# Order and pace of weight conversion and eviction in the two out products of an attention and two-MLP kernel

## The chip, the cores and the metric

The kernel runs on one core of a Trainium2 chip. The metric is the device time of one execution in microseconds; the median of three runs stands for a kernel. The trace is of one profiled execution. TensorE is called PE, VectorE DVE, ScalarE ACT, GpSimd POOL, SyncE SP.

## The reference

Sparse attention (8 heads, 2 batches of 768 positions, head size 64) is followed by two feed-forward blocks over the 1536 tokens. Only the feed-forward blocks matter here:

```python
x = attn_out.reshape(1536, 512)
xn = x / sqrt(mean(x * x) + 1e-6) * rms_g
g = xn @ w_gate                              # 512 -> 1536
x = (g * sigmoid(g) * (xn @ w_val)) @ w_out  # 1536 -> 512, the first out product
r = maximum(x @ moe2_w_in, 0)                # 512 -> 2048, the in product
out = (s * (r * r) + b) @ moe2_w_out         # 2048 -> 512, the second out product
```

The weights `w_gate`, `w_val`, `w_out`, `moe2_w_in` and `moe2_w_out` come as 64-bit words that the kernel converts itself.

## The kernel before, in words

Tokens are taken in NB = 3 blocks ("batches" in the code, index b) of 512. The width of the inner layers is taken in pieces of 128 (index f): F1 = 12 pieces for the first block, F2 = 16 for the second. Each float32 operand is split into a high and a low part, and one product is three matmuls (`mm3`, lines 183 to 186): high by high, high by low, low by high.

After the attention, `Mlp.run` goes through four stages, each a list of steps of 12 matmuls of 128x128 by 128x512:

- the gate and value products (lines 478 to 489), two steps for each (f, b);
- the first out product, weights named "o" (lines 499 to 515): 36 steps, b outermost, f inside, as `order1` says;
- the in product, weights "i" (lines 539 to 551): 48 steps, f outermost, b inside;
- the second out product, weights "p" (lines 571 to 584): 48 steps in the order of `order2`, b outermost, f inside.

A step of an out product needs three things: the converted weight of its f (`self.get`), four PSUM banks that add up over all f of one b (`acc`, banks "a" for b = 0 and 2, "gv" for b = 1), and the split of its activation tile: `split1` and `split2` write the high part on ACT and the low part on DVE. The split of step n + 1 is issued behind the matmuls of step n. It has two buffers (`side` and `ev`), which take turns, so the split of step n + 1 can begin only when step n - 1 is through on PE.

After each step, `tick(gap)` advances the weights that are in conversion by one stage each, and starts a new weight if `gap` steps have gone by since the last start. The work of one weight of 128x512 (`stages`, lines 255 to 295, in the order of `steps`) takes four ticks: (1) magnitude on ACT, floor on DVE; (2) shifts and low on DVE; (3) high on DVE, which also sets the raw buffer free and issues the load of a later weight on SP's queue; (4) `hi_part` on ACT and `lo_part` on POOL. There are three raw buffers (`raw`) and three work buffers (`cv`). Converted weights go to a ring of 8, or to a pool of their own (o with f < 4, p with f >= 8). A weight for the ring waits until an older one is dropped: in the first out product this happens in its last batch only, and so the "i" weights start at step 28 of 36. The pool for p with f >= 8 opens when the second out product begins, and so these 8 weights are converted inside that stage.

Evictions of finished sums are put off by `later(d, ...)`: to the d-th tick from there. `evac1` writes one PSUM bank as a high part (ACT) and a low part (DVE); `evac2` copies one bank to SBUF (even t on DVE, odd t on ACT) and issues its store on SP's queue.

Each engine runs its instructions in the order in which this code issues them.

Of the kernel before, what the change touches and what calls it, by code (L numbers as in the profile page):

```python
# [23 lines left out]
F1, F2 = DFF1 // 128, DFF2 // 128  # L24
BLK = 512
HB = 256
NB = B * S // BLK
# [29 lines left out]
def kernel(  # L57
# [104 lines left out]
    def open_psum(e):  # L162
        psum[:] = [e(tc.tile_pool(name="psum", bufs=1, space=PSUM))]

    def ps(kind):
        m = banks[kind][turn[kind] % len(banks[kind])]
        turn[kind] += 1
        return psum[0].tile([128, 512] if m < 8 else [128, 2, 512], F32, name=f"ps{m}", tag=f"b{m}")
# [14 lines left out]
    def mm3(o, ahi, alo, bhi, blo, first, last):  # L183
        T.matmul(out=o, lhsT=ahi, rhs=bhi, start=first, stop=False)  # L184
        T.matmul(out=o, lhsT=ahi, rhs=blo, start=False, stop=False)  # L185
        T.matmul(out=o, lhsT=alo, rhs=bhi, start=False, stop=last)  # L186


    class Mlp:
# [267 lines left out]
        def run(self, done):  # L457
            rS = ExitStack()
            open_psum(rS.enter_context)

            p1S = ExitStack()
            self.p1 = p1S.enter_context(tc.tile_pool(name="p1", bufs=NB * (F1 - G0), side="right"))
            yw = p1S.enter_context(tc.tile_pool(name="yw", bufs=F1 - RING, side="right"))
            self.xpool["o"] = (yw, lambda f: f < F1 - RING)
            parts = {}
            order1 = [(b, f) for b in range(NB) for f in range(F1)]
            y = {}

            ev1 = p1S.enter_context(tc.tile_pool(name="ev1", bufs=1, side="right"))

            def split1(n):
                b, f = order1[n]
                pt = self.pt.pop((f, b))
                phi, plo = parts[n] = self.split_tiles(n, ev1)
                A.activation(phi, pt, AF.Copy)
                V.tensor_sub(plo, pt, phi.bitcast(F32))

            for f in range(F1):
                for b in range(NB):
                    left = [c for c in (0, HB) if (f, 2 * b + c // HB) not in done]  # L480
                    if not left:
                        continue
                    c0, c1 = left[0], left[-1] + HB
                    if f == F1 - 1 and b == NB - 1:
                        split1(0)
                    for fn in self.gate_val(f, b, c0, c1, lambda: ps("gv")[:, : c1 - c0]):
                        self.later(1, fn)
                        self.tick()
                self.drop("g", f), self.drop("v", f)

            def evac1(acc, yy, m):
                yhi, ylo = yy
                A.activation(yhi[:, m, :], acc[m], AF.Copy, scale=0.5)
                V.scalar_tensor_tensor(
                    ylo[:, m, :], in0=acc[m], scalar=0.5, in1=yhi[:, m, :].bitcast(F32), op0=ALU.mult, op1=ALU.subtract
                )

            self.flush()
            for n, (b, f) in enumerate(order1):
                if f == 0:  # L500
                    acc = [ps("a" if b % 2 == 0 else "gv") for _ in range(4)]
                hi, lo = self.get("o", f)
                phi, plo = parts.pop(n)
                for m in range(4):
                    ms = slice(m * 128, (m + 1) * 128)
                    mm3(acc[m], hi[:, ms], lo[:, ms], phi, plo, f == 0, f == F1 - 1)
                if b == NB - 1:
                    self.drop("o", f)
                if n + 1 < len(order1):
                    split1(n + 1)  # L510
                if f == F1 - 1:
                    y[b] = self.new_xy()
                    for m in range(4):
                        self.later(1 + m // 2, lambda acc=acc, b=b, m=m: evac1(acc, y[b], m))
                self.tick(1)
            self.flush()
            p1S.close()
            self.p0S.close()

            gS = ExitStack()  # L520
            gp = gS.enter_context(tc.tile_pool(name="gp", bufs=NB * F2, side="right"))
            gt = {}

            def act2(o, g):
                r = self.side()
                A.activation(r, o, AF.Relu)  # L526
                V.scalar_tensor_tensor(g, in0=r, scalar=s_col, in1=r, op0=ALU.mult, op1=ALU.mult)  # L527

            def split2(n, ev=None):
                b, f = order2[n]  # L530
                g = gt.pop((f, b))
                phi, plo = parts[n] = self.split_tiles(n, ev)
                A.activation(phi, g, AF.Identity, bias=b_col)  # L533
                V.scalar_tensor_tensor(plo, in0=g, scalar=b_col, in1=phi.bitcast(F32), op0=ALU.add, op1=ALU.subtract)  # L534

            order2 = [(b, f) for b in range(NB) for f in range(F2)]
            order = [(f, b) for f in (0, 1) for b in (0, 1)] + [(0, 2), (1, 2)]
            order += [(f, b) for f in range(2, F2) for b in range(NB)]
            for f, b in order:
                hi, lo = self.get("i", f)  # L540
                yhi, ylo = y[b]
                o = ps("gv")
                for kk in range(KD):
                    mm3(o, hi[:, kk, :], lo[:, kk, :], yhi[:, kk, :], ylo[:, kk, :], kk == 0, kk == KD - 1)
                g = gt[(f, b)] = gp.tile([128, BLK], F32, name="gt", tag="gt")
                self.later(1, lambda o=o, g=g: act2(o, g))
                if b == NB - 1:
                    self.drop("i", f)
                if (f, b) == order[-1]:
                    split2(0)  # L550
                self.tick()

            self.flush()
            self.xyS.close()
            with (
                tc.tile_pool(name="ow", bufs=F2 - RING) as ow,
                tc.tile_pool(name="ev2", bufs=1, side="right") as ev2,
                tc.tile_pool(name="ob", bufs=4, side="right") as ob,
            ):
                self.xpool["p"] = (ow, lambda f: f >= RING)  # L560

                def evac2(acc, b, t):
                    o = ob.tile([128, BLK], F32, name="o", tag="o")
                    if t % 2:
                        A.activation(o, acc[t], AF.Copy)
                    else:
                        V.tensor_copy(o, acc[t])
                    r0 = self.row_of[4 * b + t]
                    nc.sync.dma_start(out[r0 : r0 + 128, :], o)

                for n, (b, f) in enumerate(order2):
                    if f == 0:
                        acc = [ps("a" if b % 2 == 0 else "gv") for _ in range(4)]
                    hi, lo = self.get("p", f)
                    phi, plo = parts.pop(n)
                    for t in range(4):
                        ts = slice(t * 128, (t + 1) * 128)
                        mm3(acc[t], phi[:, ts], plo[:, ts], hi, lo, f == 0, f == F2 - 1)
                    if n + 1 < len(order2):
                        split2(n + 1, ev2)  # L580
                    if f == F2 - 1:
                        for t in range(4):
                            self.later(1 + t // 2, lambda acc=acc, b=b, t=t: evac2(acc, b, t))
                    self.tick(1)
                self.flush()
            gS.close()
            rS.close()
# [554 lines left out]
```

## Time and profile before

| what | value |
|---|---|
| median of 3 runs | 678.24 us (677.86 to 679.38) |
| the profiled execution | 677.87 us |
| its span, first to last instruction | 676.1 us |
| PE busy | 657.4 us, 97% of the span |
| DVE busy | 408.9 us, 60% |
| ACT busy | 277.4 us, 41% |
| POOL busy | 161.1 us, 24% |
| mean granted TensorE clock | 0.995 |

Matmuls overlap, so a matmul is listed with some 390 ns although a new one begins every 227 ns. The length of a step, from its first matmul to the first of the next, is therefore a better measure than the busy time.

### The profile page before, as it was taken

What the parts mean: (1) busy time and instruction counts of PE and PEld (TensorE: products, weight loads), DVE (VectorE), ACT (ScalarE), POOL (GpSimd) and SP (SyncE); (2) the same over time, 40 slices, a digit from 0 to 9 for tenths busy, and PEclk for the clock granted to TensorE, in tenths of its full rate; (3) what the DMA queues carried; (4) which work ended last, traced back from release to release, by engine and by line L of the source; (5) the groups of instructions that cost most, each with busy time, mean ns of one, the idle gap of its engine ahead of it and who ended that gap; (6) DMA issues with size and microseconds to landing.
All of it is one profiled execution on the core that took longest, in us unless ns stands there. A gap on an engine that the chain in (4) does not pass through costs nothing.

```text
span 676.1 us, 9146 instructions
## 1 busy us (share of the span) xinstructions
PE 657.4 (97%) x3380; PEld 538.1 (80%) x3380; DVE 408.9 (60%) x847; ACT 277.4 (41%) x580; POOL 161.1 (24%) x137
## 2 busy tenths in 40 slices
PE   8999999999999999999999999999999998999996
PEld 5688888878888888888888878888888766888885
DVE  6779976336675557776324497765666798323322
ACT  3898788313332223343323344333333544322321
POOL 2476677302221112222000042211111134000000
PEclk9899999999999999999999999999999999999998
DMA  5775431003221123333000043321111231100101
GB/s 180 226 216 178 147 111 63 1 1 94 93 94 62 63 64 101 105 103 96 0 1 1 22 134 93 95 62 63 63 62 63 78 126 47 64 0 1 63 0 66
DMA packets 39940, 52.47 MB, mean 78 GB/s; under 512 B 5072, under 2 KB 31696, under 8 KB 39888
## 3 DMA queue, kind: packets, MB, share of 16 engines
q1 hardware_dynamic: 39216, 51.56, 24.1%
q8 instruction: 28, 0.46, 0.3%
q10 hardware_dynamic: 672, 0.26, 0.1%
q14 instruction: 24, 0.20, 0.1%
HBM read 48.67 MB, written 3.15 MB: 77 GB/s over the span
## 4 chain that ended last, share of the span: by engine, by line
PE 81%; DVE 8%; ACT 5%; DMA 2%; issue 2%; POOL 0%; SPq 0%; ACTq 0%; DVEq 0%; POOLq 0%
PE ps L186 26%; PE ps L184 26%; PE ps L185 25%; ACT t L810 3%; PE ps L853 1%; PE ps L782 1%; DVE t L795 1%; DVE u L277 1%; PE ps L834 1%; DMA kw<-in_k_dram 1%; DVE sm L816 1%; DVE u L271 1%; DVE ev L534 1%; DMA raw_i<-in_moe_w_in_dram 1%; DMA raw_p<-in_moe_w_out_dram 1%
## 5 line engine op out<-in xcount | busy, mean ns | idle before, releaser
L184 PE MATMUL ps<-xyh,hi_i 128*128 128x512 f32 x192 | 74.7, 389 | 0.0
L185 PE MATMUL ps<-xyl,hi_i 128*128 128x512 f32 x192 | 74.7, 389 | 0.0
L186 PE MATMUL ps<-xyh,lo_i 128*128 128x512 f32 x192 | 74.7, 389 | 0.0
L527 DVE SCALAR_TENSOR_TENSOR gt<-side,sb 128x512 f32<-128x512 f32 x48 | 38.7, 806 | 39.6 <-ACT side L526 39.6
L184 PE MATMUL ps<-xyh,hi_g 128*128 128x512 f32 (+1 forms) x160 | 60.3, 377 | 1.1 <-DVE p L924 1.1
L184 PE MATMUL ps<-xyh,hi_v 128*128 128x512 f32 (+1 forms) x160 | 60.0, 375 | 0.1
L526 ACT ACTIVATE side<-ps 128x512 f32<-128x512 f32 x48 | 28.7, 597 | 76.5 <-PE ps L186 76.5
L185 PE MATMUL ps<-xyl,hi_v 128*128 128x512 f32 (+1 forms) x160 | 58.8, 368 | 0.0
L185 PE MATMUL ps<-xyl,hi_g 128*128 128x512 f32 (+1 forms) x160 | 58.8, 368 | 0.0
L186 PE MATMUL ps<-xyh,lo_v 128*128 128x512 f32 (+1 forms) x160 | 58.8, 368 | 0.0
L186 PE MATMUL ps<-xyh,lo_g 128*128 128x512 f32 (+1 forms) x160 | 58.8, 368 | 0.0
L439 ACT ACTIVATE side<-ps 128x512 f32<-128x512 f32 x30 | 17.9, 598 | 99.1 <-PE ps L186 99.1
L290 POOL TENSOR_TENSOR lo_i<-u,hi_i 128x512 fp32r<-128x512 f32 x16 | 22.9, 1432 | 139.3 <-ACT hi_i L286 130.5
L810 ACT ACTIVATE t<-t,mn 128x232 f32<-128x232 f32 (+1 forms) x96 | 44.2, 464 | 13.0 <-DVE mn L795 12.9
L271 DVE TENSOR_SCALAR u<-u 128x512 int32<-128x512 int32 x68 | 48.7, 717 | 0.0
L821 POOL TENSOR_TENSOR t<-t,sm 128x928 f32<-128x928 f32 (+1 forms) x24 | 41.4, 1725 | 24.5 <-DVE sm L817 20.9
L440 DVE SCALAR_TENSOR_TENSOR side<-side,ps 128x512 f32<-128x512 f32 x30 | 20.6, 688 | 43.0 <-ACT side L439 43.0
L185 PEld LDWEIGHTS ps<-xyl,hi_i 128*128 128x128 f32 x192 | 36.0, 188 | 7.5
L184 PEld LDWEIGHTS ps<-xyh,hi_i 128*128 128x128 f32 x192 | 36.0, 188 | 7.5
L268 DVE TENSOR_SCALAR u<-u 128x512 f32<-128x512 f32 x68 | 39.3, 580 | 4.3 <-ACT u L264 4.3
L186 PEld LDWEIGHTS ps<-xyh,lo_i 128*128 128x128 f32 x192 | 36.0, 188 | 7.4
L534 DVE SCALAR_TENSOR_TENSOR ev<-gt,sb,ev 128x512 fp32r<-128x512 f32 x24 | 19.0, 793 | 35.0 <-ACT ev L533 35.0
(138 smaller groups left out, 1533.0 us busy)
## 6 DMA issues: line engine op xcount, KB each, us to landing
raw_i<-in_moe_w_in_dram SPq DMA_DIRECT2D x16, 512.0 KB, 3.7
raw_p<-in_moe_w_out_dram SPq DMA_DIRECT2D x16, 512.0 KB, 3.5
raw_g<-in_moe_w_gate_dram SPq DMA_DIRECT2D x12, 512.0 KB, 3.6
raw_v<-in_moe_w_val_dram SPq DMA_DIRECT2D x12, 512.0 KB, 3.6
raw_o<-in_moe_w_out_dram SPq DMA_DIRECT2D x12, 512.0 KB, 3.5
vw<-in_v_dram SPq DMA_DIRECT2D x10, 512.0 KB, 3.5
out_dram<-o SPq DMA_DIRECT2D x12, 256.0 KB, 2.3
q<-in_q_dram SPq DMA_DIRECT2D x11, 256.0 KB, 5.5
```

What stands on the lines that cost most here:

```text
L184: T.matmul(out=o, lhsT=ahi, rhs=bhi, start=first, stop=False)
L185: T.matmul(out=o, lhsT=ahi, rhs=blo, start=False, stop=False)
L186: T.matmul(out=o, lhsT=alo, rhs=bhi, start=False, stop=last)
L268: e.tensor_scalar(u, u, 2.0**-15, None, op0=ALU.max)
L271: V.tensor_scalar(ui, ui, 5, 2, op0=ALU.logical_shift_left, op1=ALU.logical_shift_right)
L290: e.tensor_tensor(lo, u, hi.bitcast(F32), op=ALU.subtract)
L440: V.scalar_tensor_tensor(th[:, :w], in0=th[:, :w], scalar=1.0, in1=g, op0=ALU.add, op1=ALU.mult)
L526: A.activation(r, o, AF.Relu)
L527: V.scalar_tensor_tensor(g, in0=r, scalar=s_col, in1=r, op0=ALU.mult, op1=ALU.mult)
L534: V.scalar_tensor_tensor(plo, in0=g, scalar=b_col, in1=phi.bitcast(F32), op0=ALU.add, op1=ALU.subtract)
L810: A.activation(t[:, hh, :], t[:, hh, :], AF.Exp, bias=mn[:, hh : hh + 1], scale=-1.0, accum_out=sm[:, hh : hh + 1])
L821: e.tensor_tensor(t, t, st["sm", g].unsqueeze(2).to_broadcast([128, 4, W]), op=ALU.mult)
```

## The change

Three things are edited, all in `Mlp.run`. In the first out product, a weight conversion starts at every second step at most in place of every step (`tick(2)`), and the four banks of a batch are evicted one at a step in place of two. In the second out product, `order2` runs f = 0 to 7 of batch 0, then f = 0 to 7 of batch 1, then f = 8 to 15 of batch 0, then f = 8 to 15 of batch 1, then all f of batch 2; the sums of batches 0 and 1 are kept in `accs` while both are open; and a conversion starts at every second step at most. The eviction of the second out product stays at two banks a step (one on each of ACT and DVE).

```diff
@@ first out product
                 if f == F1 - 1:
                     y[b] = self.new_xy()
                     for m in range(4):
-                        self.later(1 + m // 2, lambda acc=acc, b=b, m=m: evac1(acc, y[b], m))
-                self.tick(1)
+                        self.later(1 + m, lambda acc=acc, b=b, m=m: evac1(acc, y[b], m))
+                self.tick(2)
@@ second out product
-            order2 = [(b, f) for b in range(NB) for f in range(F2)]
+            order2 = [(b, f) for fs in (range(F2 // 2), range(F2 // 2, F2)) for b in (0, 1) for f in fs]
+            order2 += [(b, f) for b in range(2, NB) for f in range(F2)]
+            accs = {}
...
                     if f == 0:
-                        acc = [ps("a" if b % 2 == 0 else "gv") for _ in range(4)]
+                        accs[b] = [ps("a" if b % 2 == 0 else "gv") for _ in range(4)]
+                    acc = accs[b]
...
-                    self.tick(1)
+                    self.tick(2)
```

## Rows read from the trace of the kernel before

**Rows 1.** Busy time of PE in the page's first part.

```profile
PE 657.4 (97%) x3380; PEld 538.1 (80%) x3380; DVE 408.9 (60%) x847; ACT 277.4 (41%) x580; POOL 161.1 (24%) x137
```

**Rows 2.** Windows by stage; columns: stretch, length, busy by engine, clock, DMA.

```profile
200.00:301.99 101.99, 101.99 (x452) 84.45 (x450) 63.98 (x102) 30.78 (x53) 19.51 (x16) 1.00 0.25 81
301.99:402.11 100.12, 99.35 (x434) 80.87 (x432) 52.23 (x79) 35.58 (x61) 13.00 (x8) 1.00 0.15 44
402.11:532.67 130.56, 130.56 (x578) 108.11 (x576) 87.08 (x122) 48.81 (x86) 23.39 (x18) 1.00 0.23 72
532.67:572.12 39.45, 35.57 (x145) 26.25 (x144) 36.20 (x50) 19.68 (x32) 14.39 (x10) 1.00 0.29 94
572.12:670.20 98.08, 98.08 (x433) 80.89 (x431) 30.05 (x41) 28.17 (x40) 0.17 (x1) 1.00 0.07 24
```

**Rows 3.** Windows by step, first out product: steps 1, 33, 34, 35.

```profile
304.71:307.77 3.06, 3.01 (x14) 2.17 (x12) 3.06 (x5) 1.83 (x3) 1.28 (x1) 1.00 0.24 58
...
392.09:395.05 2.96, 2.88 (x13) 2.06 (x11) 2.93 (x5) 1.25 (x3) 1.68 (x1) 1.00 0.39 104
395.05:398.75 3.70, 3.29 (x13) 2.18 (x13) 3.67 (x7) 1.71 (x4) 1.82 (x1) 1.00 0.49 147
398.75:402.11 3.36, 3.13 (x13) 2.36 (x13) 3.33 (x6) 1.37 (x3) 1.83 (x1) 1.00 0.41 116
```

**Rows 4.** Windows by step, second out product: steps 1, 5, then 6 to 11.

```profile
535.39:538.82 3.43, 3.04 (x13) 2.18 (x12) 3.40 (x7) 1.28 (x3) 0.02 (x1) 1.00 0.00 0
...
546.98:549.70 2.72, 2.72 (x13) 2.25 (x12) 2.69 (x5) 1.83 (x3) 0.32 (x2) 1.00 0.30 81
549.70:553.21 3.51, 2.90 (x13) 2.06 (x11) 3.29 (x6) 1.33 (x3) 1.34 (x1) 1.00 0.43 121
553.21:556.53 3.32, 3.26 (x12) 2.10 (x12) 3.29 (x4) 1.82 (x4) 1.33 (x1) 1.00 0.34 138
556.53:560.55 4.02, 3.29 (x13) 2.10 (x12) 3.99 (x7) 1.80 (x4) 1.78 (x1) 1.00 0.48 140
560.55:564.29 3.74, 3.32 (x12) 2.10 (x12) 3.71 (x6) 1.81 (x4) 1.51 (x1) 1.00 0.36 130
564.29:567.67 3.38, 3.13 (x13) 2.28 (x13) 3.35 (x5) 1.72 (x3) 1.53 (x2) 1.00 0.00 0
567.67:572.12 4.45, 3.02 (x13) 2.18 (x12) 3.25 (x4) 1.35 (x2) 2.56 (x2) 1.00 0.01 2
```

**Rows 5.** Instructions on the raw tiles of p: ns min/median/max, first, last start.

```profile
L264 ACT ACTIVATE u<-raw_p x16: 657/668/687, 476.8 to 562.9; 128x512 f32<-128x512 f32 x16
L274 DVE SCALAR_TENSOR_TENSOR u<-raw_p,u x16: 691/693/694, 480.3 to 567.3; 128x512 int32<-128x512 int32 x16
L277 DVE SCALAR_TENSOR_TENSOR u<-raw_p,u x16: 677/686/1783, 482.5 to 569.6; 128x512 int32<-128x512 int32 x16
...
DMA to landing us min/median/max: 3.4/3.5/4.3
```

**Rows 6.** Timelines of ACT, DVE and POOL, 538.7 to 572.2: start, length, instruction, wait.

```profile
562.95 0.68 ACT L264 ACTIVATE u<-raw_p 128x512 f32<-128x512 f32 x1 [1.93 <-DMA raw_p<-in_moe_w_out_dram]
563.09 0.41 DVE L271 TENSOR_SCALAR u<-u 128x512 int32<-128x512 int32 x1
564.14 0.42 DVE L268 TENSOR_SCALAR u<-u 128x512 f32<-128x512 f32 x1
564.15 0.62 ACT L286 ACTIVATE hi_p<-u 128x512 fp32r<-128x512 f32 x1
564.48 0.74 DVE L534 SCALAR_TENSOR_TENSOR side<-gt,sb,side 128x512 fp32r<-128x512 f32 x1
567.66 1.45 POOL L290 TENSOR_TENSOR lo_p<-u,hi_p 128x512 fp32r<-128x512 f32 x1 [1.29 <-ACT hi_p L286]
567.89 1.77 DVE L534 SCALAR_TENSOR_TENSOR ev<-gt,sb,ev 128x512 fp32r<-128x512 f32 x1
572.15 0.72 ACT L533 ACTIVATE ev<-gt,sb 128x512 fp32r<-128x512 f32 x1 [1.23 <-PE ps L185]
```

## The prediction

> **What bounds the kernel now.** I read the page's busy times first: PE is busy for 657.4 us, 97% of the span [rows 1]. A change that keeps the number of matmuls can win only where PE stands still, so the next view is the windows by stage, to see where that is. The in product is the yardstick: its 48 steps take 130.56 us with PE busy all the time, 2.72 us a step of 12 matmuls, at a granted clock of 1.00, the upper level of 2.4 GHz [rows 2]. Against it, the first out product's 36 steps should take 97.92 us and take 100.12, 2.20 too many. The second one's steps 0 to 11 should take 32.64 us and take 39.45, 6.81 too many; its later 36 steps take 98.08, within 0.2 us of 36 x 2.72 = 97.92 [rows 2]. The gate and value stage before them has PE busy all the time. So the stages that the change touches hold 2.20 + 6.81 = 9.01 us of standstill, 1.3% of the time, and no more can be won.
>
> The windows by step put a place on each part. In the first out product four steps are over 2.72: step 1 by 0.34, and steps 33, 34 and 35 by 0.24, 0.98 and 0.64 [rows 3]; they add up to the whole 2.20, so all other steps, those with evictions too, lose nothing. In the second, step 1 loses 0.71, and steps 6 to 11 lose 0.79, 0.60, 1.30, 1.02, 0.66 and 1.73, together 6.10 [rows 4]. These are the steps in which one weight after another is converted.
>
> Why they lose is a count of DVE's work. One weight costs DVE floor 0.42, shifts 0.41, low 0.69 and high 0.69, 2.21 us in all, and the split of the step 0.74 [rows 5, 6]: 2.95 us, more than a step of 2.72 has, when a weight goes through in every step. POOL makes it worse: a `lo_part` ran from 567.66 for 1.45 us, and the split that DVE began 0.23 us later took 1.77 us in place of 0.74; `high` has a median of 0.69 and a longest of 1.78 [rows 5, 6]. The third part is the load: it is issued by `high` and lands 3.5 us later (median), longer than a step; ACT's magnitude waited 1.93 us for it at 562.95, and the split's ACT half stands behind it in ACT's queue [rows 5, 6]. In the losing steps DVE is busy for 3.25 to 3.99 us of 3.32 to 4.45 [rows 4].
>
> **The change part by part.** *Pace in the second out product.* No instruction is added or removed; the 8 weights p8 to p15 are spread from a start in every step (1 to 8) to a start in every second step (1, 3, to 15). I followed the code's ticks by hand. p8 is finished at step 4 as before, p15 at step 18 (before: 11). The new order needs p8 at step 16, and p15 at step 23: a margin of 5 steps at the least, where the old order would have needed p15 at step 15. So the slower pace is paid for by the new order, and `get` never has to force a conversion.
>
> What a pair of steps now holds, from its start at 0: ACT's split half 0 to 0.72, DVE's half to 1.46; ACT's `hi_part` 0.72 to 1.34, so POOL's `lo_part` 1.34 to 2.79; DVE's shifts begin at 1.46, stand behind POOL until 2.79 and end at 3.20, low at 3.89; in the second step ACT's half runs 2.72 to 3.44 and DVE's half 3.89 to 4.63, then high to 5.32 and floor to 5.74 [rows 5, 6]. Each split is ready before its step must begin (1.46 against 2.72, 4.63 against 5.44), by 1.26 and 0.81 us. The DVE sum with the standstill is 2.21 + 2 x 0.74 + 1.33 = 5.02 of 5.44 us. Loads have four steps, 10.9 us, from `high` to the magnitude that needs them, against 3.5 [rows 5], so ACT's queue is clear as well. Steps 6 to 11 lose nothing any more: minus 6.10.
>
> Step 1 stays. Up to it the two versions issue the same instructions in the same order on every engine: the split of step 1 goes out at step 0, behind the last ReLU and square of the in product and p7's magnitude and floor. Its 0.71 us remains [rows 4].
>
> *Pace in the first out product.* At step 28 the ring frees its first place. Before, a weight starts in each of steps 28 to 35; now at 28, 30, 32 and 34. That is the same pair of steps as above, so steps 33 to 35 lose nothing: minus 1.86 [rows 3]. The bill goes to the in product, which finds three weights converted at its start in place of five. It needs weight f at step 3f (from f = 2 on), and gets i3 at step 1, i4 at 3, then one every second step: i3 with 8 steps to spare, and more for each later one. That stage carries 87 us of DVE work in 130.56 [rows 2] and more of it moves to its first 22 steps; its PSUM banks take turns by four, which hides a late eviction for 3 steps, some 8 us. I cost it at nothing; without that cover, each late step would cost like those of rows 4, 0.6 to 1.7 us. From its step 22 on both versions issue the same. Step 1 of this stage stays too (0.34): the split that it waits for is queued before the two versions differ. Weights o10 and o11 are finished by step 5 and needed at step 10.
>
> *Evictions of the first out product.* Four pairs of ACT and DVE instructions are spread from two steps to four. The steps that hold them lose nothing now, since the four steps listed carry the stage's whole 2.20 us [rows 3], so nothing is won. In the last batch three of the four now come in the `flush` ahead of the in product, ahead of its first evictions; they are read by the in product's step 4, 10.9 us later. Cost nothing.
>
> *Order and banks.* Batches 0 and 1 hold all eight banks from step 8 to step 23. The "gv" banks were last used by the in product, whose last eviction is issued at step 0; batch 2 takes "a" at step 32, 8 steps after batch 0 was evicted. Batch 0's stores go out at steps 23 and 24 in place of 15 and 16; on SP's queue they now follow the loads of all weights, the last of which moves from step 7 to 11. Batch 1's and batch 2's stores, and so the tail of the kernel, stay where they were. Whether a sum that is left half done for 8 steps costs PE anything, no row shows. The nearest one is that banks change every three matmuls now at no cost, in 2.72 us steps [rows 2], so I take nothing.
>
> *Sum.* 6.10 + 1.86 = 7.96 us go, 1.05 stay. The profiled execution took 677.87 (its span is 676.1, and 1.8 lies around it): 677.87 - 7.96 = 669.91. The median of the runs lies 0.37 higher than this execution, so I say 670.1, between the two bases. Bounds of what is unsure: at best the two step 1 stalls go as well, 677.87 - 9.01 = 668.9. At worst a pair of steps is less clean than worked out; the smallest standstill of rows 3 and 4, 0.24 us, for each of the 11 weights converted beside splits (p8 to p15, i0 to i2) is 2.6 us: 672.5. I take nothing for it, because step 5 of the second out product holds 2.69 us of DVE work in 2.72 and loses nothing [rows 4].
>
> **A rule against it.** The row of 567.89 shows DVE held until POOL is through [rows 6]. The Trainium skill (SBUF — State Buffer, section "SBUF: two separate sides") states why: the port pair of GpSimd and VectorE is an exclusive lock, held for a whole instruction, and the loser blocks fully, as VectorE operations with two SBUF inputs do. By that rule the change lifts no lock: each weight still has its `lo_part`, whatever the pace. The trace agrees (1.77 for 0.74). By the row alone the lock is one step's accident and the sum stays 669.9; by the rule it can come back with every weight, which is the slower rival below.
>
> **The rivals.** *The lock takes the split, and it is slower.* If POOL's `lo_part` begins before DVE's split, the split is held, and PE waits for it: step 11 lost 1.73 that way [rows 4, 6]. At 11 weights this is 19.0 us, and 677.87 - 7.96 + 19.0 = 688.9. It decides from 7.96 / 11 = 0.72 us a weight. For it speaks that the lock is seen; against it that `hi_part`, and so `lo_part`, stands behind the split's ACT half in ACT's queue, 0.62 us after it, and that DVE has 0.4 us to spare in a pair of steps.
>
> *The lock takes a part.* Half of the slower price, or the mean of the nine standstills (0.88) for the 8 weights p8 to p15, is 7.1 us: 677.0. Between this and 672.5 lies a lock that hits some weights alone.
>
> *It doesn't do what it says.* If ACT's wait for the loads sets the second stage [rows 6] and does so at any pace, only the 1.86 of the first goes: 676.0. Against it: the wait stands because `high` is late and the next magnitude comes one step behind, which the new pace ends.
>
> **How the numbers follow.** The forecast (669.3 to 671) has 0.75. A start without the step 1 stalls, 668.9: 0.04. The lock in part: 0.12, about half of it below 672.5. Not as it says, 676.0: 0.05. Slower, 688.9: 0.04. The range 668.8 to 672.5 holds some 0.85. Within 0.2% (1.4 us, about what a measurement of this kernel can tell from no change) lies only the end of the partial lock, 0.03; faster 0.93, slower 0.04.
>
> **What would show it.** In the trace of after: windows by step of 2.72 for steps 2 to 23 of the second out product, and for steps 28 to 35 of the first; step 1 still at 3.4 and 3.1; no wait of ACT for a raw tile of p; the in product at 130.6 in all, as before. A split of 1.8 us with a step over 3 us behind it would speak for the lock, an in product over 131 for weights or evictions that come late, a step 16 or later over 2.72 for conversions that the new order needs too early.

## The result, and the profile after

The changed kernel takes 668.51 us (668.41 to 669.33) beside 678.05 us of the kernel before, a ratio of 0.9872 with a 95% interval of 0.9855 to 0.989. The ratio is an estimate from all the runs of both kernels; the quotient of the two medians is 0.9859. The forecast was 670.1 in a range of 668.8 to 672.5, a ratio of 0.988 to the 678.24 that it started from: the ratios agree, and the median lies 0.3 us below the lower end of the range, which the part on why the prediction was right takes up. The profiled execution after took 669.33 us with a span of 667.4, against 677.87 and 676.1.

The windows by stage of the changed kernel (stretch, length, busy time of PE, PEld, DVE, ACT, POOL, then clock and DMA) answer to [rows 2]: the first out product, the in product, steps 0 to 11 of the second out product, and the rest of it.

```profile
301.20:399.46 98.26, 98.21 (x433) 81.01 (x432) 47.10 (x71) 34.15 (x59) 9.13 (x7) 1.00 0.12 38
399.46:530.02 130.56, 130.56 (x577) 108.11 (x576) 94.50 (x129) 50.17 (x88) 25.48 (x20) 1.00 0.25 77
530.02:562.67 32.65, 32.26 (x142) 26.38 (x141) 27.18 (x38) 16.23 (x26) 7.92 (x6) 1.00 0.29 97
562.67:661.45 98.78, 98.78 (x436) 81.46 (x434) 39.12 (x54) 31.36 (x46) 5.34 (x4) 1.00 0.08 29
```

The first out product went from 100.12 to 98.26, minus 1.86, to the hundredth what was forecast, since the forecast was that steps 33 to 35 lose nothing at all. The in product is unchanged at 130.56, though DVE works 7.4 us more in it. The third window ends inside a step, so the second out product is best taken whole: 131.43 from 530.02 to 661.45, against 137.53 from 532.67 to 670.20 before, minus 6.10. The three stages together, from the first matmul of the first out product to the end of the last matmul: 368.21 before, 360.25 after, minus 7.96.

The windows by step answer to [rows 3] and [rows 4]: steps 1, 33, 34 and 35 of the first out product, then steps 1, 7 and 8 of the second.

```profile
303.92:306.98 3.06, 3.01 (x13) 2.17 (x12) 3.06 (x5) 1.27 (x2) 1.28 (x1) 1.00 0.25 44
...
391.30:394.02 2.72, 2.72 (x13) 2.25 (x12) 1.82 (x3) 1.16 (x2) 1.23 (x1) 1.00 0.64 193
394.02:396.74 2.72, 2.72 (x13) 2.25 (x12) 2.51 (x4) 1.20 (x2) 0.33 (x1) 1.00 0.00 0
396.74:399.46 2.72, 2.72 (x13) 2.25 (x12) 1.17 (x3) 1.84 (x4) 0.59 (x1) 1.00 0.66 196
532.75:536.17 3.42, 3.03 (x13) 2.18 (x13) 3.38 (x7) 1.28 (x3) 0.02 (x1) 1.00 0.00 0
...
549.77:552.49 2.72, 2.72 (x13) 2.25 (x12) 2.49 (x5) 1.31 (x3) 0.00 (x0) 1.00 0.00 0
552.49:555.21 2.72, 2.72 (x13) 2.25 (x12) 1.99 (x2) 1.22 (x2) 1.33 (x1) 1.00 0.60 193
```

Only the two steps 1 are still long, as forecast (3.06 and 3.43 before). The steps where a weight is converted now hold 2.49 and 1.99 us of DVE work in turn, in place of up to 3.99 in one.

The pair of steps that the prediction laid out can be read in the timelines of DVE and POOL; step 4 of the second out product starts at 541.61 and step 5 at 544.33.

```profile
542.34 0.75 DVE L534 SCALAR_TENSOR_TENSOR ev<-gt,sb,ev 128x512 fp32r<-128x512 f32 x1 [0.92 <-ACT ev L533]
543.01 1.51 DVE L271 TENSOR_SCALAR u<-u 128x512 int32<-128x512 int32 x1
545.17 0.74 DVE L534 SCALAR_TENSOR_TENSOR side<-gt,sb,side 128x512 fp32r<-128x512 f32 x1
...
542.90 1.33 POOL L290 TENSOR_TENSOR lo_p<-u,hi_p 128x512 fp32r<-128x512 f32 x1 [4.09 <-ACT hi_p L286]
```

The split of step 5 ends at 543.09, 1.48 us into the pair (laid out: 1.46), that of step 6 at 545.91, 4.30 into it (laid out: 4.63); both are early for their steps at 2.72 and 5.44. POOL still holds DVE once for each weight: from step 2 on the instruction that stands is now the shifts, eight times (1.51 or 1.52 us, against 0.41 in [rows 6]), where it was `high` or the split in the losing steps before. It is not that the shifts can be held for nothing: in the kernel before, they were the ones held in the first out product too, and steps 33 to 35 lost 1.86 us there. What is new is that a hold is followed by two steps' time in place of one. The first row is from the timeline of DVE before, in step 34; the second answers to the longest `high` in [rows 5], in the list of instructions on p's raw tiles after:

```profile
396.24 1.51 DVE L271 TENSOR_SCALAR u<-u 128x512 int32<-128x512 int32 x1
...
L277 DVE SCALAR_TENSOR_TENSOR u<-raw_p,u x16: 684/684/689, 479.8 to 578.5; 128x512 int32<-128x512 int32 x16
```

### The profile page after: what moved, and what is told of

It is laid out like the page before. It is cut to its first block, busy times and chain, and to the rows that moved or that the text cites. A ratio compares the mean times of both kernels' runs of the same rounds, so it can differ in the third digit from the quotient of the medians.

```text
span 667.4 us, 9155 instructions
## 1 busy us (share of the span) xinstructions
PE 652.7 (98%) x3380; PEld 538.2 (81%) x3380; DVE 411.4 (62%) x847; ACT 277.3 (42%) x580; POOL 158.0 (24%) x137
## 4 chain that ended last, share of the span: by engine, by line
PE 87%; DVE 5%; ACT 4%; DMA 1%; issue 1%; POOL 0%; DVEq 0%; POOLq 0%; ACTq 0%
PE ps L184 27%; PE ps L186 27%; PE ps L185 27%; ACT t L814 3%; PE ps L786 2%; PE ps L857 1%; DVE t L799 1%; PE ps L838 1%; DVE sm L820 1%; DMA words<-in_n_local_dram 1%; PE ps L176 1%; ACT pt L845 1%; DVE u L277 1%; DMA raw_g<-in_moe_w_gate_dram 0%; DVE xn L402 0%
## 5 line engine op out<-in xcount | busy, mean ns | idle before, releaser
L271 DVE TENSOR_SCALAR u<-u 128x512 int32<-128x512 int32 x68 | 61.8, 911 | 0.0
L527 DVE SCALAR_TENSOR_TENSOR gt<-side,sb 128x512 f32<-128x512 f32 x48 | 36.1, 751 | 33.5 <-ACT side L526 33.5
L290 POOL TENSOR_TENSOR lo_i<-u,hi_i 128x512 fp32r<-128x512 f32 x16 | 21.4, 1339 | 136.3 <-ACT hi_i L286 132.1
L290 POOL TENSOR_TENSOR lo_p<-u,hi_p 128x512 fp32r<-128x512 f32 x16 | 21.0, 1314 | 85.7 <-ACT hi_p L286 80.9
```

The costliest lines, as they stand in the source:

```text
L271: V.tensor_scalar(ui, ui, 5, 2, op0=ALU.logical_shift_left, op1=ALU.logical_shift_right)
L290: e.tensor_tensor(lo, u, hi.bitcast(F32), op=ALU.subtract)
```

## The experiments

**Each half of the change alone.** The first run undoes the edits in the first out product, the second those in the second.

```diff
 # e1_p_only, against the changed kernel
-                        self.later(1 + m, lambda acc=acc, b=b, m=m: evac1(acc, y[b], m))
-                self.tick(2)
+                        self.later(1 + m // 2, lambda acc=acc, b=b, m=m: evac1(acc, y[b], m))
+                self.tick(1)
 # e2_o_only, against the kernel before
-                        self.later(1 + m // 2, lambda acc=acc, b=b, m=m: evac1(acc, y[b], m))
-                self.tick(1)
+                        self.later(1 + m, lambda acc=acc, b=b, m=m: evac1(acc, y[b], m))
+                self.tick(2)
```

> The second out product as changed (order by halves, a conversion at every second step), the first out product as before. Theory of the pace (DVE and ACT have more than a step's work when a weight goes through in every step): the steps 6 to 11 of the second out product fall to 2.72 us and 6.1 us go against the kernel before, while steps 33 to 35 of the first still lose 1.9. Theory that POOL's low part takes the gain back at every weight: steps over 3 us stay between 2 and 18, and less than 3 us go. A gain of over 7 us would say that something outside the out products is faster.

> The first out product as changed (a conversion at every second step, one eviction a step), the second as before. Theory of the pace: steps 33 to 35 of the first out product fall to 2.72 us, 1.9 us go against the kernel before, the in product stays at 130.6 us. Rival, that the weights of the in product come late: its 48 steps take over 131 us and the 1.9 are given back.

e1_p_only took 671.36 us, a ratio of 0.9905 (0.9882 to 0.9928), and e2_o_only 675.44 us, 0.9961 (0.9946 to 0.9975), beside 677.57 of the kernel before. Windows by stage of e1_p_only (first out product and second out product):

```profile
301.09:401.12 100.03, 99.38 (x434) 80.85 (x433) 52.16 (x79) 35.58 (x61) 12.99 (x8) 1.00 0.15 45
...
531.67:663.14 131.47, 131.08 (x577) 107.84 (x575) 66.31 (x91) 47.58 (x72) 13.23 (x10) 1.00 0.13 46
```

and of e2_o_only (all three):

```profile
302.12:400.38 98.26, 98.21 (x434) 81.00 (x433) 47.11 (x71) 34.14 (x59) 9.13 (x7) 1.00 0.12 38
400.38:530.93 130.55, 130.55 (x577) 108.11 (x576) 94.49 (x129) 50.17 (x88) 25.47 (x20) 1.00 0.24 77
530.93:668.18 137.25, 133.69 (x577) 107.14 (x575) 66.18 (x91) 47.89 (x72) 14.21 (x10) 1.00 0.13 44
```

The halves are independent. The second out product alone gives 137.53 - 131.47 = 6.06, the first alone 1.86; the in product stays at 130.55 with the late weights, so nothing is given back there.

**The order without the pace, and the pace without the order.**

```diff
 # e3_order_only, against e1_p_only
-                    self.tick(2)
+                    self.tick(1)
 # e4_pace_only, against the kernel before, second out product
-                    self.tick(1)
+                    self.tick(2)
```

> The order by halves alone, a conversion still at every step, the first out product as before. Theory of the pace: the weights were not late, the splits were, so steps 6 to 11 of the second out product lose some 6 us as before and the time is that of the kernel before within 0.5 us. Rival, that PE waited for weights needed too soon: the standstill of steps 6 to 11 goes, minus 6 us.

> A conversion at every second step in the second out product, in the old order, the first out product as before. The code then has to force p12 to p15, which are not through when they are needed. Theory: steps 6 to 11 fall to 2.72 us (minus 6.1), but steps 12 to 15 wait for conversions that begin late, 2 to 4 us each for p14 and p15: plus 4 to 8, so between 2 us faster and 2 us slower than the kernel before. Rival, that the order is not needed: 6 us faster with no step over 2.72 from 12 to 15.

e3_order_only took 677.74 us, 1.0 (0.9985 to 1.0016); e4_pace_only 678.64 us, 1.0013 (0.9998 to 1.0027). Windows of e3_order_only, steps 8 and 11:

```profile
556.38:560.33 3.95, 3.33 (x13) 2.09 (x13) 3.92 (x7) 1.80 (x4) 1.75 (x1) 1.00 0.44 141
...
567.51:571.94 4.43, 3.02 (x13) 2.17 (x12) 3.24 (x4) 1.36 (x2) 2.53 (x2) 1.00 0.00 2
```

These are the lengths of [rows 4]: with the order alone, six steps lose what they lost, so PE didn't wait for weights but for splits. Whatever PE waits for in these steps of the kernel before, by its waits, is a half of a split. In e4_pace_only steps 6 to 10 are at 2.72 each, and the loss has moved to where the weights are needed. Its windows, steps 12 to 15, and the waits of PE in that stretch (who waited for whom: us, times, longest):

```profile
566.39:570.38 3.99, 3.14 (x12) 2.33 (x13) 3.08 (x4) 1.21 (x2) 1.40 (x2) 1.00 0.39 131
570.38:575.04 4.66, 3.18 (x13) 2.02 (x13) 3.06 (x5) 1.96 (x4) 1.15 (x1) 1.00 0.00 0
575.04:580.61 5.57, 4.71 (x12) 3.49 (x13) 3.41 (x5) 1.85 (x4) 2.00 (x2) 0.69 0.00 0
580.61:583.84 3.23, 3.02 (x13) 2.17 (x12) 1.42 (x2) 1.22 (x2) 0.56 (x1) 1.00 0.11 36
...
PE ps L185 <- POOL lo_p L290: 2.7, 4, 0.9
```

Steps 11 to 15 lose 0.18, 1.27, 1.94, 2.85 and 0.51, together 6.75, where 6.10 was won. The expectation had p15 as costly as p14, and it was not: 0.51. Of the 2.85 us of step 14, 1.4 are a lower clock (last section). In this stage neither edit gives anything alone; together they give 6.1.

**Which of the three causes: DVE's work, POOL's lock, or the loads.** The prediction named all three without shares. These runs take the lock or the loads, or both, from the kernel before.

```diff
 # e5_no_lo (lo_part and its tile left out for p8 to p15)
+                if kind == "p" and f >= RING:
+                    lo = hi
+                else:
                     e.tensor_tensor(lo, u, hi.bitcast(F32), op=ALU.subtract)
 # e6_no_load (in load(); rawx is loaded once ahead of step 0)
+            if kind == "p" and f >= 10:
+                self.raws[(kind, f)] = self.rawx
+                self.loaded += 1
+                return
 # e7_neither: both
```

> The kernel before, with the low part of the weights p8 to p15 left out (the high part is used in its place), so POOL does nothing in steps 4 to 11 of the second out product; DVE's 2.95 us a step and the loads stay. If POOL's lock on DVE is what takes a step over its length, the standstill of steps 6 to 11 (6.1 us) falls under 2 us. If the late loads do it, 4 us or more stay, and ACT still waits some 2 us for raw tiles of p.

> The kernel before, with p10 to p15 converted from one raw tile that is loaded once when the second out product begins; their six loads are left out, so ACT has nothing to wait for. If the late loads take a step over its length, the standstill of steps 6 to 11 falls under 2 us. If DVE's work with POOL's lock does it (2.95 + about 1.1 us a step), 4 us or more stay.

> The kernel before without the low parts of p8 to p15 and without the loads of p10 to p15, as in the two runs above together. DVE still has 2.95 us a step of 2.72. By the count of DVE's work alone some 8 x 0.23 = 1.8 us are over, of which the slack of a split (about 1 us) hides half: a standstill of 0 to 1 us in steps 6 to 11. Over 3 us would say that a third thing, neither lock nor load, sets these steps.

e5_no_lo took 672.62 us, 0.9939 (0.992 to 0.9959); e6_no_load 677.07, 0.9995 (0.9981 to 1.0009); e7_neither 670.78, 0.9906 (0.9876 to 0.9936). Windows of e5_no_lo, steps 6 and 7, and ACT's waits in the stage:

```profile
548.62:551.89 3.27, 2.88 (x13) 2.06 (x11) 2.23 (x6) 1.32 (x3) 0.00 (x0) 1.00 0.43 152
551.89:555.08 3.19, 3.13 (x13) 2.28 (x14) 3.16 (x6) 2.29 (x4) 0.00 (x0) 1.00 0.22 74
...
ACT u L264 <- DMA raw_p<-in_moe_w_out_dram: 7.9, 5, 2.3
```

Windows of e6_no_load, steps 7, 8 and 11, ACT's waits (its lines are four further down), and DVE's timeline from one floor to the next:

```profile
551.34:555.08 3.74, 3.19 (x13) 2.07 (x12) 3.71 (x6) 1.79 (x4) 1.84 (x1) 1.00 0.00 0
555.08:558.85 3.77, 3.22 (x13) 2.10 (x12) 3.74 (x6) 1.83 (x4) 1.83 (x1) 1.00 0.00 0
...
566.24:570.70 4.46, 3.01 (x13) 2.17 (x12) 3.27 (x4) 1.36 (x2) 2.56 (x2) 1.00 0.01 2
...
ACT u L268 <- POOL lo_p L294: 9.6, 5, 2.0
...
551.47 0.42 DVE L272 TENSOR_SCALAR u<-u 128x512 f32<-128x512 f32 x1
...
552.47 1.78 DVE L281 SCALAR_TENSOR_TENSOR u<-rawx,u 128x512 int32<-128x512 int32 x1
...
555.23 0.42 DVE L272 TENSOR_SCALAR u<-u 128x512 f32<-128x512 f32 x1
```

The row that ACT's wait answers to, in the same steps of the kernel before (532.6 to 572.2):

```profile
ACT u L264 <- DMA raw_p<-in_moe_w_out_dram: 10.2, 5, 2.3
```

One window of e7_neither, from the first matmul of step 6 to that of step 12, and again two floors in a row on DVE:

```profile
547.90:564.22 16.32, 16.32 (x73) 13.52 (x72) 13.34 (x25) 9.46 (x15) 0.00 (x0) 1.00 0.00 0
...
551.23 0.42 DVE L272 TENSOR_SCALAR u<-u 128x512 f32<-128x512 f32 x1
...
553.89 0.42 DVE L272 TENSOR_SCALAR u<-u 128x512 f32<-128x512 f32 x1
```

Against 6.10 us of standstill in steps 6 to 11 of the kernel before, 1.99 are left without the low parts (steps 6 to 10 lose 0.55, 0.47, 0.46, 0.46 and 0.05), 5.78 without the loads, and none without either (16.32 = 6 x 2.72). POOL's low part is the main cause. In e6_no_load DVE is busy in all but 0.03 us of each of steps 7 and 8, so DVE with what POOL holds it is the bound there: from floor to floor it takes 3.76 us, with `high` at 1.78 in place of 0.69. The loads are a second cause that lies under the first: without them ACT waits about as long for a work buffer that POOL's low part gives back (9.6 us) as it waited for the loads before (10.2 us), and they show only once POOL is out of the way.

DVE's own work alone is not a cause. With neither POOL nor loads, the floor of one weight begins 2.66 us after that of the one before it, with the shifts, low, high and a split in between. That is less than a step of 2.72 us. The 2.95 us of the prediction and the expectations are a sum of listed lengths, and on DVE a listed length reaches into the next instruction, as it does with the matmuls: the floor at 551.23 is listed with 0.42 us, and the split behind it began at 551.56.

e5_no_lo takes away two things at once, POOL's hold on DVE and POOL's late return of the work buffers; how the 4.1 us share between these two is open, and was not tried. That DVE hardly idles in steps 7 to 10 of the kernel before (0.03 us each [rows 4]) speaks for the hold, but no run shows it alone.

**The evictions.**

```diff
 # e9_evac_pairs, against the changed kernel
-                        self.later(1 + m, lambda acc=acc, b=b, m=m: evac1(acc, y[b], m))
+                        self.later(1 + m // 2, lambda acc=acc, b=b, m=m: evac1(acc, y[b], m))
```

> The changed kernel, with the evictions of the first out product back at two a step. Prediction: nothing changes, all steps 11 to 14 and 23 to 26 at 2.72 us with either. Rival, that the pairs delay the splits: these steps lose some tenths each, at most 1 us in all.

It took 669.57 us, 0.9882 (0.9861 to 0.9904) of the kernel before. The window over its first out product:

```profile
301.96:400.22 98.26, 98.21 (x434) 81.00 (x432) 47.28 (x70) 34.28 (x59) 8.53 (x6) 1.00 0.12 38
```

98.26 us as in the changed kernel: evicting one bank a step is worth nothing.

**The two stalls that are left.**

```diff
 # e8_first_splits, against the changed kernel
                         split1(0)
+                        split1(1)
...
-                if n + 1 < len(order1):
+                if 0 < n < len(order1) - 1:
                     split1(n + 1)
...
-                self.tick()
+                self.tick(0 if (f, b) == order[-1] else 2)
 # e11_quiet_step, against e8_first_splits (tick(None) leaves out the conversions)
-                self.tick(0 if (f, b) == order[-1] else 2)
+                self.tick(None if (f, b) == order[-1] else 2)
```

> The changed kernel, with the two stalls that are left taken away: the second split of the first out product is issued together with its first one, before the last two steps of the gate stage, and no weight is started in the last step of the in product, so that p7's magnitude and floor no longer stand ahead of the second split. Theory (these stalls are queueing ahead of the split): step 1 of both out products falls to 2.72 us, 0.34 + 0.71 = 1.05 us go against the changed kernel. Rival, that a stage's first steps wait for its PSUM banks or weights: step 1 stays at 3.06 and 3.43.

> The changed kernel again, beside the run above on the same chip. If its gain beyond the 7.96 us of the out products was the scatter of the part before 300 us, the time from the first instruction to the first out product differs by up to 1 us from run to run and the median gain comes out between 7.5 and 9.5 us. If the change moved that part, its start of the first out product is earlier than the kernels with the old order in every profile.

> The run with the first splits moved (e8), where the second split of the second out product took 1.33 us behind POOL's low part of p6 and step 1 lost 0.31 us; now no conversion is advanced in the last step of the in product, so that p6's high and low part come behind that split. If POOL's lock is what held it, the split takes 0.75 us, step 1 falls to 2.72 us and the three stages take 0.3 us less (359.2 in place of 359.5). If the split waits for something else, step 1 stays at 3.03. The time by median can't tell 0.3 us.

On one chip, e8_first_splits took 669.04 us (667.51 to 669.6), 0.9885 (0.9864 to 0.9906), and the changed kernel again, e10_after, 669.48 (668.6 to 669.94), 0.9891 (0.9871 to 0.9911). e11_quiet_step took 668.94 (668.35 to 670.11), 0.9883 (0.9866 to 0.9901). These three can't be told apart by the time; their stages can. e8_first_splits, windows of the first out product's step 1 and the second's step 1, then the timelines of DVE and POOL around the second split:

```profile
304.80:307.52 2.72, 2.72 (x13) 2.25 (x12) 2.67 (x5) 1.16 (x2) 1.17 (x1) 1.00 0.29 79
533.28:536.31 3.03, 3.02 (x14) 2.17 (x12) 2.60 (x5) 0.73 (x2) 0.03 (x1) 1.00 0.00 0
...
532.52 1.33 DVE L535 SCALAR_TENSOR_TENSOR ev<-gt,sb,ev 128x512 fp32r<-128x512 f32 x1 [0.38 <-ACT ev L534]
...
532.01 1.30 POOL L290 TENSOR_TENSOR lo_p<-u,hi_p 128x512 fp32r<-128x512 f32 x1 [6.87 <-ACT hi_p L286]
```

The first stall (0.34) is gone, of the second (0.71) 0.31 is left, so 0.74 of the expected 1.05 us went: now the split stands behind POOL's low part of p6, which began 0.51 us ahead of it. With that low part moved behind the split, e11_quiet_step shows the split at 0.74 us, and its windows by stage are:

```profile
302.53:400.45 97.92, 97.92 (x434) 81.08 (x432) 46.70 (x70) 33.56 (x58) 9.40 (x7) 1.00 0.12 38
400.45:531.01 130.56, 130.56 (x578) 108.11 (x576) 94.50 (x129) 50.01 (x88) 25.41 (x20) 1.00 0.24 77
531.01:661.73 130.72, 130.72 (x577) 107.92 (x575) 66.34 (x91) 47.58 (x72) 13.28 (x10) 1.00 0.13 46
...
532.51 0.74 DVE L536 SCALAR_TENSOR_TENSOR ev<-gt,sb,ev 128x512 fp32r<-128x512 f32 x1
```

With that, PE is busy all the time in all three stages: 359.20 us, 1.05 less than the changed kernel and 9.01 less than the kernel before, which is the whole standstill that the prediction counted.

## Why the prediction was right

*The sum.* The three stages lost 7.96 us, as forecast: 1.86 and 6.10, with the in product and the two steps 1 unchanged. That it comes out to the hundredth is no finer knowledge of the steps: the forecast was that nine standstills, read from the trace, go as a whole, and they went. What the forecast took at nothing did cost nothing: the order and the half done sums (all steps from 2 on at 2.72 us), the evictions (e9_evac_pairs), the in product's later weights (e2_o_only).

*The basis.* The measured gain was 9.54 us beside one set of runs of the kernel before (678.05 to 668.51) and 7.76 beside another (677.24 to 669.48, e10_after). In the profiles the first out product starts at 301.20 in the changed kernel's first profile and at 302.22 in its second, so the part ahead of it, which no experiment changes before its last steps, scatters by a microsecond; over all the profiles it lies between 300.23 and 302.53, early and late with either order. The forecast's 670.1 was 1.6 too long by the first basis, and the median of 668.51 fell 0.3 below its range; the median of e10_after, 669.48, is inside it. The sum of the stages was not what was off. The range was: its lower end was worked out from the two steps 1 alone and gave nothing to the scatter ahead of the stages, though the runs of the kernel before on record lay 1.5 us apart.

*The pace.* The theory that a split is late because a weight goes through in every step holds: in the second out product order alone gives nothing, pace alone gives nothing, since the old order needs the weights too soon.

*The count.* The reason that the prediction put first, that a weight and a split are 2.95 us of DVE work and so more than a step, was wrong. Start to start they are 2.66 us, and e7_neither runs at that pace without a standstill. What it put second, as what "makes it worse", is what makes DVE too slow: POOL's hold adds 1.1 us to each round of one weight and one split, 3.76 in all, and that is the length of steps 7 and 8 in e6_no_load (3.74 and 3.77). Nor was the hold one step's accident, as the prediction has it by the row alone. In the timeline of DVE before, `high` was held for 1.77 or 1.78 us six times, from 546.05 to 565.14; the median over all 16 weights in [rows 5] hides this, and a list of the stretch from 546.98 to 572.12 shows it:

```profile
L277 DVE SCALAR_TENSOR_TENSOR u<-raw_p,u 128x512 int32<-128x512 int32 x7 | 11.4, 1622 | 0.0
```

The forecast came right all the same, because two steps, 5.44 us, have room for the work and the hold by either count. Adding up listed lengths is also part of why the second split of the pair came 0.33 us earlier than laid out (4.30 for 4.63); the rest is that POOL's low part ended 0.17 us earlier than laid out (2.62 for 2.79).

*The third cause.* The prediction put the loads beside DVE and POOL as a cause of their own, on the strength of ACT's waits. e6_no_load shows that taking them away leaves 5.78 of 6.10 us. ACT's wait for the loads was the wait that came last in a loop where another wait was as long. The sum didn't need this step, since the change mends both.

*The slower rival.* It didn't come. The lock does come back with every weight: the shifts of p8 to p15 are held each time (1.51 us for 0.41). That it can take a split and that PE pays for it is shown by e8_first_splits (0.31 us) and by its absence in e11_quiet_step. The rule cited from the Trainium skill (SBUF — State Buffer, section "SBUF: two separate sides") stands: the change lifts no lock. What it does is to leave each hold two steps to be made up in, and a queue in which no split stood behind POOL.

## What to carry to other kernels

When an engine that isn't the bound lets the bound one stand still, count its work by step of the bound engine, with the time that another engine holds it, and not by its share of the span: here DVE was at 60% and was still too slow for six steps in a row. Count it from start to start in a dense stretch, not as a sum of listed lengths (2.66 us here, not 2.95). A slower pace for side work is worth its whole backlog only if the main loop gives it that time: the in product had it to spare, so in the first out product the pace was enough; in the second, pace and order each gave nothing alone. And before a wait is named as the cause, take it away: if another of the same length takes its place, it was one of several in a loop.

## What the runs showed of the hardware

In e4_pace_only the granted clock of TensorE fell inside a dense stretch. By the timeline of PE it had been idle for 0.85, 0.80, 0.68 and 0.86 us ahead of four matmuls between 567.75 and 576.40, and then seven matmuls in a row began 427 ns after the one ahead of them, in place of 227: the granted clock is 0.50, the lower level of 1.2 GHz. Windows of that stretch:

```profile
576.40:577.40 1.00, 1.00 (x4) 0.84 (x5) 0.97 (x3) 0.00 (x0) 0.00 (x0) 0.88 0.00 0
577.40:578.40 1.00, 1.00 (x4) 0.81 (x3) 0.97 (x2) 0.00 (x0) 0.00 (x0) 0.50 0.00 0
578.40:579.40 1.00, 1.00 (x4) 0.71 (x4) 0.71 (x2) 0.22 (x1) 0.00 (x0) 0.50 0.00 0
579.40:580.40 1.00, 1.00 (x4) 0.81 (x3) 0.00 (x0) 0.41 (x1) 0.51 (x1) 0.50 0.00 0
580.40:581.40 1.00, 0.79 (x4) 0.33 (x3) 0.13 (x1) 0.72 (x1) 0.77 (x1) 0.92 0.02 8
```

These seven cost 7 x 0.2 = 1.4 us of that run's 6.75. In the kernel before, the longest idle time of PE in steps 6 to 11 was longer, 1.43 us:

```profile
569.71 0.50 PE L186 MATMUL ps<-hi_p,ev 128*128 128x512 f32 x1 [1.43 <-DVE ev L534]
```

The others were shorter (0.61 us at most), and the clock stayed at 1.00 in every one of these steps [rows 4]. In these two profiles, then, the late weights cost the clock beside their waits and the late splits did not. It is one profile of each kernel, and no run shows what would bring the clock down in general.
